# Attention kernel: a two-bank PSUM tile that is opened at step 3 and closed after the last step with three maxima, and another rotation of the late heads' banks

## The chip, the cores and the metric

The kernel runs on one core of a Trainium2 chip. The metric is the device time of one execution in microseconds (us); the median of three runs stands for a kernel. The core has TensorE (PE, matmuls; its weight loads are shown apart as PEld), VectorE (DVE), ScalarE (ACT, here the exponentials), GpSimd (POOL) and SyncE (SP, which issues the transfers). Matmul results land in PSUM, here used as eight banks of 128 partitions x 512 float32.

## The reference

Two attention blocks read the same x (2048 tokens, 448 features, 16 heads of 28) and a gate mixes them:

```python
g = _sigmoid((x * gate_w).sum(-1, keepdims=True))
a = _A_ref(x, A_wqkv, A_w_phi, A_wo)      # linear attention with a softmax feature map
b = _B_ref(x, B_wqkv, B_wo)               # below
return g * a + (1 - g) * b

# _B_ref
scores = jnp.einsum("bhqd,bhkd->bhqk", q, k) * scale
p = _softmax(scores, axis=-1)
o = jnp.einsum("bhqk,bhkd->bhqd", p, v)
return (o, heads joined) @ wo
```

All of it is float32, and the kernel keeps that precision by splitting numbers into a high and a low part.

## The kernel before

The first 350 us project x, do the linear attention of block A and prepare q, k and v of block B in device memory. The change touches none of that. From then on runs the softmax attention of block B, in 256 steps. A step s is one key tile of 128 tokens (kt, 16 of them) for one block of 512 queries (qb, 4 of them) of one group of four heads (g, 4 of them).

In a step PE computes, for the four heads, the scores transposed (128 keys x 512 queries), each in three passes that add into one PSUM bank (line 878, `score`: high x high, low x high, high x low). Each head uses 32 rows of the array, so matmuls of different heads run side by side. ACT takes the exponential of each finished bank (`exps_of`: line 887 for two banks at once, line 890 for one). Two steps later PE multiplies the exponentials with v (line 1033, `values`, the tile `pv`); that work uses the array in four column strips instead of four row strips.

The exponential needs a number per query to subtract. It is a maximum over keys, which is computed ahead of the group that needs it: further matmuls (line 288, `mx_score`), each with a reduction on DVE (line 295, `mx_done`). There are 704 of these, three in each of the steps 1 to 234 and two in step 235. From step 236 on a step has scores only. At six of the late steps (237, 239, 244, 246, 252, 254) PE also does two output projections, called pob (line 109 through `project`), each followed by one DVE instruction that adds the result into `acc` (line 1044). After step 255 the last block is finished in `finish_last`.

Eight banks are all there is. One holds `pv`. In before the other seven are five single tiles g2 to g6 and one tile named `wide` that is two banks; bank number 0 and bank number 1 in the code are its halves. All exist until the end of the kernel. In a step with three maxima the seven banks are given out in this order: two heads whose scores start first (e0 and e1), the first two maxima, two heads whose scores start later (l0 and l1), the third maximum. From step 2 on e0 and e1 have the two halves of `wide`, so that one exponential of 1024 columns serves both. The other five come from the list `ring`, which is permuted at every step. Step 1 runs on single exponentials, and one of its maxima is written into a half of `wide`. In the steps without three maxima, and for pob, the banks come from the front of the list `free`, so that halves of `wide` are used there one by one.

The order within a step is written out in `scores`: first pass of e0 and e1, the first two maxima; second pass of e0 and e1, first pass of l0 and l1; third pass of e0 and e1, second pass of l0 and l1; third pass of l0 and l1; the third maximum. Each engine works through its own queue in the order of the program. Semaphore waits are placed by the tile layer, per tile: a bank that is given out anew is a new tile and waits for the last reader of the old one, whereas `wide` is one tile for the whole kernel, and readers and writers of its halves are ordered as those of one object.

Of the kernel before, what the change touches and what calls it, by code (L numbers as in the profile page):

```python
# [8 lines left out]
F32 = mybir.dt.float32  # L9
# [5 lines left out]
PSUM = bass.MemoryType.PSUM  # L15
DRAM = bass.MemoryType.DRAM

P = 128
# [23 lines left out]
def gated_mix_kernel(ctx, tc, xT, wqkB, wvB, wvA, wkAT, wqAT, phi, woA, woB,  # L42
# [15 lines left out]
    ps = ps_s_.enter_context(tc.tile_pool(name="ps", bufs=1, space=PSUM, reuse_waits="tile"))  # L58
# [226 lines left out]
    def mx_score(item, pm):  # L285
        gq, kb, qt, j, _ = item
        js = slice(32 * j, 32 * j + DH)
        nc.tensor.matmul(pm, mxs[("qc", gq)][js, qt * P:(qt + 1) * P],  # L288
                         mxs[("kc", gq // NQ, kb)][js, :], start=True, stop=True,
                         tile_position=(32 * j, 0))  # L290

    def mx_done(item, pm):
        gq, kb, qt, h, col = item
        g, qb = divmod(gq, NQ)
        nc.vector.tensor_reduce(part[:, col:col + 1], pm, AX.X, ALU.max)  # L295
        if h < 3:
            return
        if kb == 1 and qt == 0 and gq + 1 < NG * NQ:
            mx_query(gq + 1)
        if qb == NQ - 1 and g + 1 < NG:  # L300
            if qt == 2 and kb == 3:
                mx_load(g + 1, 0)
            if qt == 3 and kb < 3:
                mx_load(g + 1, kb + 1)
        if qt == 3 and kb == 3:
            mx_reduce(gq)
# [404 lines left out]
    for i in range(2 * NT + 11):  # L711
# [15 lines left out]
        if q == 2:  # L727
# [7 lines left out]
            ps = ps_s_.enter_context(tc.tile_pool(name="psq", bufs=1, space=PSUM, reuse_waits="tile"))  # L735
# [18 lines left out]
        if q in (7, 10):  # L754
            b = 2 + q // 10
# [60 lines left out]
        if q == NT + 6:  # L816
            ps_s_.close()
            ps = ps_s_.enter_context(tc.tile_pool(name="psv", bufs=1, space=PSUM, reuse_waits="tile"))
# [51 lines left out]
    pv_of, pts, late, mids = {}, {}, {}, {}  # L870
    PASSES = ((0, 0), (1, 0), (0, 1))

    def score(s, j, n, st):

        gq, kt = divmod(s, NT)
        k, q = PASSES[n]
        js = slice(32 * j, 32 * j + 32)
        nc.tensor.matmul(st[j], kst_of[(gq // NQ, kt // 4)][js, k, (kt % 4) * P:(kt % 4 + 1) * P],  # L878
                         qst_of[gq][js, q, :], start=n == 0, stop=n == 2,
                         tile_position=(32 * j, 0), skip_group_check=True)  # L880

    def exps_of(s, js, st, wide=None):
        pw = late_p.tile([P, 2, 512], F32, tag="pw", name=f"pw{s}", bufs=4)
        pts[s] = {j: pw[:, i] for i, j in enumerate(js[:2])}
        pts[s].update({j: late_p.tile([P, 512], F32, tag="p", name=f"p{s}_{j}", bufs=8) for j in js[2:]})
        if wide is not None:
            nc.scalar.activation(pw, wide, AF.Exp, scale=SCALE)  # L887
            js = js[2:]
        for j in js:
            nc.scalar.activation(pts[s][j], st[j], AF.Exp, scale=SCALE)  # L890
# [11 lines left out]
    def scores(s, todo):  # L902

        if len(todo) == 3:
            l0, l1, e0 = [x[3] for x in todo]
            e1, = {0, 1, 2, 3} - {l0, l1, e0}
            order = [1, 2, 0, 3, 4, 5, 6] if s == 1 else [0, 1] + ring
            b = [bank(i, f"g{s}_{n}") for n, i in enumerate(order)]  # L910
            st, pm = {e0: b[0], e1: b[1], l0: b[4], l1: b[5]}, [b[2], b[3], b[6]]
            m0, m1, r0, r1, m2 = ring
            ring[:] = [3, 2, 6, 4, 5] if s == 1 else [m0, m1, r0, m2, r1]
            free[:] = [m0, m1, 0, 1, r0, m2, r1]
            for n in range(4):
                for j in (e0, e1) if n < 3 else ():
                    score(s, j, n, st)
                for i, j in enumerate((l0, l1)):
                    if n:
                        score(s, j, n - 1, st)  # L920
                    else:
                        mx_score(todo[i], pm[i])
            mx_score(todo[2], pm[2])
            js = [e0, e1, l0, l1]
        else:
            js = [0, 1, 2, 3]
            n = 4 + len(todo)
            b = free[:n]
            free[:] = free[n:] + b[4:] + b[:4]
            b = [bank(i, f"g{s}_{n}") for n, i in enumerate(b)]  # L930
            st, pm = dict(enumerate(b[:4])), b[4:]
            for n in range(3):
                for j in js:
                    score(s, j, n, st)
            for x, m in zip(todo, pm):
                mx_score(x, m)
        exps_of(s, js, st, wide if len(todo) == 3 and s > 1 else None)
        for x, m in zip(todo, pm):
            mx_done(x, m)

# [22 lines left out]
    take_acts()  # L963
    ps_s_.close()
    fr_s.close()
    ps2 = ctx.enter_context(tc.tile_pool(name="ps2", bufs=1, space=PSUM, reuse_waits="tile"))

    free, ring = [], [2, 3, 4, 5, 6]

    def bank(i, nm):
        if i < 2:
            return wide[:, i]
        return ps2.tile([P, 512], F32, tag=f"g{i}", name=nm, bufs=1)

    def take_bank(nm):
        free.append(free.pop(0))
        return bank(free[-1], nm)  # L980

    ps2.tile([P, 512], F32, tag="pv", name="pv_first", bufs=1)
    for i in (2, 6, 5, 4, 3):
        bank(i, f"first{i}")
    wide = ps2.tile([P, 2, 512], F32, tag="wide", name="wide", bufs=1)

    late_p = ctx.enter_context(tc.tile_pool(name="late", bufs=1, reuse_waits="tile"))
    woB_s = late_p.tile([P, 2, 4, D], F32R, name="woB_s")
# [37 lines left out]
    def values(s):  # L1026
        gq, kt = divmod(s, NT)
        g, qb = divmod(gq, NQ)
        if kt == 0:
            pv_of[gq] = ps2.tile([P, 512], F32, tag="pv", name=f"pv{gq}", bufs=1)  # L1030
        pv, pt = pv_of[gq], pts.pop(s)
        for j in range(4):
            nc.tensor.matmul(pv[32 * j:32 * j + 32, :], vb[kt // 8][:, kt % 8, 4 * g + j, :],  # L1033
                             pt[j],
                             start=kt == 0, stop=kt == NT - 1, tile_position=(0, 32 * j),
                             skip_group_check=True)
# [124 lines left out]
    for s in range(NS + 18):  # L1161
        gq, kt = divmod(s, NT)
        g, qb = divmod(gq, NQ)
# [18 lines left out]
        if 0 < s < NS:  # L1182
            if s in mids:
                mids.pop(s)()
            scores(s, mx_next())
# [4 lines left out]
        while vals and vals[0] <= upto:  # L1190
            t = vals.pop(0)
            values(t)
            if t % NT == NT - 1:
                finish(t // NT, s)
# [74 lines left out]
```

## Time and profile before

| what | us |
|---|---|
| median of 3 runs | 975.44 (975.02 to 976.71) |
| the profiled execution | 975.22 |
| its span | 973.4 |
| PE busy | 963.1 (99%) |
| ACT busy | 737.0 (76%) |
| DVE busy | 716.4 (74%) |
| POOL busy | 231.5 (24%) |

A timeline row gives start, duration, engine, line, operation, what is written and read, how many instructions are merged into the row, and in brackets how long the engine had been idle and what ended that. A releaser is inferred, and "issue" means that the engine waited for nothing that the profile shows. The profiled execution lies 0.22 us under the median, and 1.82 us of it lie outside the span.

### The profile page before, as it was taken

How to read it: one execution, taken by the hardware profiler on the slowest of the kernel's cores; microseconds unless marked ns; L12 is line 12 of the kernel's file. 1: busy time of each engine (PE TensorE's matmuls, PEld its weight loads, DVE VectorE, ACT ScalarE, POOL GpSimd, SP SyncE). 2: the span in 40 equal slices, each digit the busy share in tenths (PEclk: the TensorE clock that was granted, in tenths of full speed). 3: DMA queues.
4: the chain of work that ended last, by engine and by line, in shares of the span. 5: the costliest groups of instructions: out<-in, count | busy, mean ns of one | idle time of the engine just before them, and what ended most of it. 6: DMA issues, size and time to landing. Idle time of an engine off the chain costs nothing.

```text
span 973.4 us, 22367 instructions
## 1 busy us (share of the span) xinstructions
PE 963.1 (99%) x8510; PEld 573.3 (59%) x8510; DVE 716.4 (74%) x1338; ACT 737.0 (76%) x1209; POOL 231.5 (24%) x237
## 2 busy tenths in 40 slices
PE   9999999999999999999999999999999999999998
PEld 8877877787877654444444444444444444445555
DVE  5476767788845778888888888888888888884112
ACT  4465655588866788888888888888888888886561
POOL 1235435578634700121101101001101101100010
PEclk9999999999999999999999999999999999999999
DMA  9883111023233333022132022132132123000441
GB/s 301 307 266 118 36 54 33 35 62 87 85 107 104 110 107 125 22 59 60 51 103 72 22 62 60 51 87 73 51 84 60 51 59 94 13 21 31 151 144 57
DMA packets 56619, 84.48 MB, mean 87 GB/s; under 512 B 17696, under 2 KB 24464, under 8 KB 56512
## 3 DMA queue, kind: packets, MB, share of 16 engines
q1 hardware_dynamic: 56512, 83.06, 28.4%
q8 instruction: 67, 1.10, 0.5%
q14 instruction: 40, 0.33, 0.1%
HBM read 54.86 MB, written 27.78 MB: 85 GB/s over the span
## 4 chain that ended last, share of the span: by engine, by line
PE 99%; ACT 0%; DVE 0%; issue 0%; POOL 0%; DVEq 0%; POOLq 0%; ACTq 0%
PE pv L1033 26%; PE wide L878 18%; PE g L878 9%; PE pqk L109 6%; PE g L288 5%; PE poa L109 4%; PE pk L127 4%; PE pva L127 4%; PE pq L109 4%; PE pmd L260 4%; PE pvb L127 2%; PE pvb L109 2%; PE pob L109 2%; PE pft L521 2%; PE pqk L635 1%; PE wide L109 1%
## 5 line engine op out<-in xcount | busy, mean ns | idle before, releaser
L295 DVE TENSOR_REDUCE part<-g 128x1 f32<-128x512 f32 x703 | 441.8, 684 | 77.5 <-PE g L288 74.8
L887 ACT ACTIVATE pw<-wide 128x1024 f32<-128x1024 f32 x233 | 238.7, 1024 | 65.8 <-PE wide L878 64.6
L1033 PE MATMUL pv<-p,vb 128*32 128x512 f32 x1028 | 270.4, 604 | 0.0
L890 ACT ACTIVATE p<-g 128x512 f32<-128x512 f32 x495 | 269.2, 602 | 0.0
L1033 PE MATMUL pv<-pw,vb 128*32 128x512 f32 x1020 | 268.9, 604 | 0.0
L878 PE MATMUL g<-qst,kst 32*128 32x512 f32 x1587 | 245.7, 419 | 0.0
L878 PE MATMUL wide<-qst,kst 32*128 32x512 f32 x1473 | 240.8, 427 | 4.4 <-DVE acc L1044 1.7
L878 PEld LDWEIGHTS wide<-qst,kst 32*128 32x128 f32 x1473 | 119.6, 182 | 202.4 <-ACT pw L887 191.7
L288 PE MATMUL g<-kc,qc 28*128 28x512 f32 x703 | 231.8, 492 | 0.1
L878 PEld LDWEIGHTS g<-qst,kst 32*128 32x128 f32 x1587 | 128.3, 183 | 37.4 <-ACT pw L890 8.4
L265 DVE CUSTOM_DVE_ANT_0 rl<-pmb,rl 128x512 f32<-128x512 f32 x160 | 103.4, 684 | 50.7 <-ACT rl L264 50.7
L405 POOL TENSOR_TENSOR oUb<-oUb,rsb 128x512 f32<-128x512 f32 x15 | 19.3, 1287 | 488.6 <-DMA rsb<-rdb 356.8
L264 ACT ACTIVATE rl<-pmd 128x512 f32<-128x512 f32 x160 | 87.3, 601 | 31.1 <-PE pmb L260 29.6
L288 PEld LDWEIGHTS g<-kc,qc 28*128 28x128 f32 x703 | 86.4, 181 | 0.5 <-DVE part L295 0.4
L109 PE MATMUL pqk<-XH,wB 128*128 128x512 f32 x192 | 59.1, 396 | 0.0
L1033 PEld LDWEIGHTS pv<-pw,vb 128*32 128x32 f32 x1020 | 37.6, 108 | 36.1 <-issue 35.4
L1033 PEld LDWEIGHTS pv<-p,vb 128*32 128x32 f32 x1028 | 37.9, 108 | 31.8 <-issue 31.1
L573 ACT CAST ev<-pqk 128x512 fp32r<-128x512 f32 x28 | 16.0, 589 | 38.7 <-PE pqk L109 23.3
L109 PE MATMUL poa<-woA_s,oTa 128*128 128x448 f32 x192 | 43.4, 374 | 0.0
L574 DVE TENSOR_TENSOR ev<-pqk,ev 128x512 fp32r<-128x512 f32 x28 | 19.0, 689 | 30.7 <-ACT ev L573 30.7
L260 PE MATMUL pmb<-kp,qp 28*128 28x512 f32 x160 | 41.2, 495 | 0.0
L109 PEld LDWEIGHTS pqk<-XH,wB 128*128 128x128 f32 x192 | 35.4, 188 | 8.5 <-issue 1.2
(182 smaller groups left out, 1254.6 us busy)
## 6 DMA issues: line engine op xcount, KB each, us to landing
qkd<-ev SPq DMA_DIRECT2D x28, 512.0 KB
qst<-qkd SPq DMA_DIRECT2D x64, 112.0 KB
kst<-qkd SPq DMA_DIRECT2D x64, 112.0 KB
od<-oTb SPq DMA_DIRECT2D x48, 112.0 KB
rsa<-rda SPq DMA_DIRECT2D x32, 128.0 KB
oL<-od SPq DMA_DIRECT2D x8, 512.0 KB
rsb<-rdb SPq DMA_DIRECT2D x15, 256.0 KB
gad<-ga SPq DMA_DIRECT2D x16, 224.0 KB
```

What stands on the lines that cost most here:

```text
L109: nc.tensor.matmul(dst, l, r, start=i == 0, stop=i == len(todo) - 1)
L127: nc.tensor.matmul(dst[:, :n], l, r, start=i == 0, stop=i == len(todo) - 1, skip_group_check=True)
L260: nc.tensor.matmul(pm[j], qc[js, qt * P:(qt + 1) * P], kc[js, :], start=True, stop=True, tile_position=(32 * i, 0))
L264: nc.scalar.activation(rl, pm[i], AF.Relu)
L265: nc.vector.tensor_tensor_reduce(rl, pm[2 + i], rl, 1.0, LOWEST, ALU.add, ALU.max, part[:, col + i:col + i + 1])
L288: nc.tensor.matmul(pm, mxs[("qc", gq)][js, qt * P:(qt + 1) * P], mxs[("kc", gq // NQ, kb)][js, :], start=True, stop=True, tile_position=(3 ...
L295: nc.vector.tensor_reduce(part[:, col:col + 1], pm, AX.X, ALU.max)
L521: nc.tensor.transpose(p[:, (n - a) * P:(n - a + 1) * P], f[:, 2 * n:2 * n + 2].rearrange("p e c -> p (e c)"), ident)
L878: nc.tensor.matmul(st[j], kst_of[(gq // NQ, kt // 4)][js, k, (kt % 4) * P:(kt % 4 + 1) * P], qst_of[gq][js, q, :], start=n == 0, stop=n == ...
L887: nc.scalar.activation(pw, wide, AF.Exp, scale=SCALE)
L890: nc.scalar.activation(pts[s][j], st[j], AF.Exp, scale=SCALE)
L1033: nc.tensor.matmul(pv[32 * j:32 * j + 32, :], vb[kt // 8][:, kt % 8, 4 * g + j, :], pt[j], start=kt == 0, stop=kt == NT - 1, tile_position ...
```

## The change

The tile `wide` no longer exists from the start to the end. `pv` moves to a pool of its own (`ps1`). The other seven banks are in a pool that is opened three times by the new function `open_banks`: for steps 1 and 2 with seven single tiles, from step 3 with five single tiles and `wide` (now banks 3 and 2), and from step 235 with seven single tiles again. The order in which the first tiles are taken keeps each bank number at the same place in each of the pools.

Steps 1 and 2 have single exponentials for all four heads (one more step than before), and step 2 takes its banks from `free`. In the steps with `wide` the permutation of `ring` is another one. Before, l0 of a step got the bank that l0 had in the step before, l1 got that of the third maximum, and the third maximum that of l1. Now l0 gets the bank of the third maximum, l1 that of l0, and the third maximum that of l1, as before. The matmuls and their order in a step are the same; of the exponentials one pair becomes two single ones.

```diff
@@ scores(s, todo)
-            order = [1, 2, 0, 3, 4, 5, 6] if s == 1 else [0, 1] + ring
-            b = [bank(i, f"g{s}_{n}") for n, i in enumerate(order)]
+            if s == 3:
+                open_banks(3, True)
+            if s < 3:
+                b = free[:]
+                free[:] = [b[2], b[0], b[3], b[1], b[6], b[4], b[5]]
+            else:
+                b = [3, 2] + ring
+                m0, m1, r0, r1, m2 = ring
+                ring[:] = [m0, m1, m2, r0, r1]
+                free[:] = [m0, m1, 3, 2, m2, r0, r1]
+            b = [bank(i, f"g{s}_{n}") for n, i in enumerate(b)]
             st, pm = {e0: b[0], e1: b[1], l0: b[4], l1: b[5]}, [b[2], b[3], b[6]]
-            m0, m1, r0, r1, m2 = ring
-            ring[:] = [3, 2, 6, 4, 5] if s == 1 else [m0, m1, r0, m2, r1]
-            free[:] = [m0, m1, 0, 1, r0, m2, r1]
...
         else:
+            if banks["wide"] is not None:
+                open_banks(4, False)
...
-        exps_of(s, js, st, wide if len(todo) == 3 and s > 1 else None)
+        exps_of(s, js, st, banks["wide"] if len(todo) == 3 else None)
@@ after the first part of the kernel
-    ps2 = ctx.enter_context(tc.tile_pool(name="ps2", bufs=1, space=PSUM, reuse_waits="tile"))
-    free, ring = [], [2, 3, 4, 5, 6]
+    ps1 = ctx.enter_context(tc.tile_pool(name="ps1", bufs=1, space=PSUM, reuse_waits="tile"))
+    ps1.tile([P, 512], F32, tag="pv", name="pv_first", bufs=1)
+    free, ring = [0, 1, 2, 3, 4, 5, 6], [1, 0, 5, 6, 4]
+    banks = {}
+
+    def open_banks(n, pair):
+        if banks:
+            banks["s"].close()
+        banks.update(s=ctx.enter_context(ExitStack()), wide=None)
+        banks["ps"] = banks["s"].enter_context(
+            tc.tile_pool(name=f"ps{n}", bufs=1, space=PSUM, reuse_waits="tile"))
+        for i in (0, 6, 5, 4, 3, 2, 1):
+            if not pair or i not in (2, 3):
+                bank(i, f"first{n}_{i}")
+            elif i == 3:
+                banks["wide"] = banks["ps"].tile([P, 2, 512], F32, tag="wide", name="wide", bufs=1)
 
     def bank(i, nm):
-        if i < 2:
-            return wide[:, i]
-        return ps2.tile([P, 512], F32, tag=f"g{i}", name=nm, bufs=1)
+        if banks["wide"] is not None and i in (2, 3):
+            return banks["wide"][:, 3 - i]
+        return banks["ps"].tile([P, 512], F32, tag=f"g{i}", name=nm, bufs=1)
...
-    ps2.tile([P, 512], F32, tag="pv", name="pv_first", bufs=1)
-    for i in (2, 6, 5, 4, 3):
-        bank(i, f"first{i}")
-    wide = ps2.tile([P, 2, 512], F32, tag="wide", name="wide", bufs=1)
+    open_banks(2, False)
```

Three places in the instruction order show it. In the rows, g_0 to g_6 are the single tiles by their position in the step (a number behind the position only tells tiles apart), `kc` and `qc` are the operands of the maxima, `qst` and `kst` those of the scores, and the brackets name the engines whose semaphores the instruction waits for.

The first place is DVE at step 1, where it begins the reductions of the maxima. Before:

```order
L230 TENSOR_REDUCE red<-part 128x4x4 [waits DVE_49]
L857 STREAM_TRANSPOSE nm_4471<-red 128x128 [waits DVE_49]
L295 TENSOR_REDUCE part<-wide 128x1 [waits Activation_49]
L295 TENSOR_REDUCE part<-g_3_4474 128x1 [waits PE_49]
L295 TENSOR_REDUCE part<-g_6_4477 128x1 [waits PE_49]
```

And now:

```order
L230 TENSOR_REDUCE red<-part 128x4x4 [waits DVE_49]
L857 STREAM_TRANSPOSE nm_4475<-red 128x128 [waits DVE_49]
L295 TENSOR_REDUCE part<-g_2_4479 128x1 [waits PE_49]
L295 TENSOR_REDUCE part<-g_3_4480 128x1 [waits PE_49]
L295 TENSOR_REDUCE part<-g_6_4483 128x1 [waits PE_49]
```

The first maximum stood in a half of `wide` and its reduction waited for ACT; it now stands in a tile of its own and waits for PE.

The second place is PE in a step with three maxima in the middle of the attention: the first matmuls of step 233. Before:

```order
L878 MATMUL wide<-qst_4016,kst_4042 128x512 [waits Activation_49]
L878 MATMUL wide<-qst_4016,kst_4042 128x512
L288 MATMUL g_2_12711<-kc_2_9693,qc_11400 128x512 [waits DVE_49]
L288 MATMUL g_3_12712<-kc_2_9693,qc_11400 128x512 [waits DVE_49]
L878 MATMUL wide<-qst_4016,kst_4042 128x512 x2
L878 MATMUL g_4_12713<-qst_4016,kst_4042 128x512 [waits Activation_49]
L878 MATMUL g_5_12714<-qst_4016,kst_4042 128x512 [waits DVE_49]
```

And now:

```order
L878 MATMUL wide<-qst_4016,kst_4042 128x512 [waits Activation_49]
L878 MATMUL wide<-qst_4016,kst_4042 128x512
L288 MATMUL g_2_12730<-kc_2_9712,qc_11419 128x512 [waits DVE_49]
L288 MATMUL g_3_12731<-kc_2_9712,qc_11419 128x512 [waits DVE_49]
L878 MATMUL wide<-qst_4016,kst_4042 128x512 x2
L878 MATMUL g_4_12732<-qst_4016,kst_4042 128x512 [waits DVE_49]
L878 MATMUL g_5_12733<-qst_4016,kst_4042 128x512 [waits Activation_49]
```

The two late heads (g_4 is l0, g_5 is l1) have exchanged what they wait for; nothing else is moved.

The third place is PE at step 237, where the second of two projections is followed by the scores. Before:

```order
L109 MATMUL pob_12846<-woB_s,oTb_0_12292 128x448 [waits Pool_49]
L109 MATMUL wide<-woB_s,oL_11551 128x448 [waits Activation_49]
L109 MATMUL wide<-woB_s,oL_11551 128x448 x7
L109 MATMUL wide<-woB_s,oTb_0_12292 128x448 x3
L878 MATMUL wide<-qst_4016,kst_4018 128x512 [waits DVE_49]
L878 MATMUL g_1_12873<-qst_4016,kst_4018 128x512 [waits Activation_49]
```

And now:

```order
L109 MATMUL pob_12878<-woB_s,oTb_0_12311 128x448 [waits Pool_49]
L109 MATMUL pob_12892<-woB_s,oL_11570 128x448 [waits Activation_49]
L109 MATMUL pob_12892<-woB_s,oL_11570 128x448 x7
L109 MATMUL pob_12892<-woB_s,oTb_0_12311 128x448 x3
L878 MATMUL g_0_12906<-qst_4016,kst_4018 128x512 [waits Activation_49]
L878 MATMUL g_1_12907<-qst_4016,kst_4018 128x512 [waits Activation_49]
```

The first score had one half of `wide` while the projection had the other, and waited for DVE; it now has a tile of its own and waits for an exponential.

More of the change, by code (lines that the diff above doesn't have):

```diff
@@ L1029, in values @@
         if kt == 0:
-            pv_of[gq] = ps2.tile([P, 512], F32, tag="pv", name=f"pv{gq}", bufs=1)
+            pv_of[gq] = ps1.tile([P, 512], F32, tag="pv", name=f"pv{gq}", bufs=1)
         pv, pt = pv_of[gq], pts.pop(s)
```

## The prediction, made before the result

> **What bounds the kernel now.** I read the page first, then the waits of PE over the whole span, then the timelines of three places: the first steps, a step in the middle, and the last 90 us.
>
> ```profile
> span 973.4 us, 22367 instructions
> PE 963.1 (99%) x8510; PEld 573.3 (59%) x8510; DVE 716.4 (74%) x1338; ACT 737.0 (76%) x1209; POOL 231.5 (24%) x237
> PE 99%; ACT 0%; DVE 0%; issue 0%; POOL 0%; DVEq 0%; POOLq 0%; ACTq 0%
> ```
>
> PE carries 99% of the chain that ended last, and it is busy for all but 10.3 us. No matmul is removed, so the change can only fill gaps in PE or move the rhythm of the steps. These are the gaps that PE's own view names:
>
> ```profile
> PE wide L878 <- DVE acc L1044: 1.7, 2, 0.8
> ...
> PE wide L878 <- ACT p L890: 1.2, 1, 1.2
> PE wide L878 <- DVE part L295: 1.2, 1, 1.2
> PE wide L109 <- DVE acc L1044: 0.8, 1, 0.8
> PE wide L878 <- ACT pw L887: 0.3, 2, 0.2
> ```
>
> Columns are total us, times, longest. All five are matmuls that write the tile `wide`. Four of the five come where the change takes `wide` away: step 2 (DVE part) and the steps from 235 on (acc twice on line 878, once on line 109, and p). The weight loads show the gaps better, since there the length of an ordinary gap can be read too.
>
> **The start, steps 1 to 3.**
>
> ```profile
> 350.50 0.60 ACT L890 ACTIVATE pw<-wide 128x512 f32<-128x512 f32 x1
> 351.48 1.09 ACT L890 ACTIVATE p<-g 128x512 f32<-128x512 f32 x2
> 353.63 1.02 ACT L887 ACTIVATE pw<-wide 128x1024 f32<-128x1024 f32 x1 [1.06 <-PE wide L878]
> ...
> 349.52 0.50 PE L288 MATMUL g<-kc,qc 28*128 28x512 f32 x1
> ...
> 351.13 0.69 DVE L295 TENSOR_REDUCE part<-wide 128x1 f32<-128x512 f32 x1 [2.79 <-ACT pw L890]
> ...
> 351.88 0.18 PEld L878 LDWEIGHTS wide<-qst,kst 32*128 32x128 f32 x2 [1.60 <-DVE part L295]
> 353.98 0.16 PEld L1033 LDWEIGHTS pv<-p,vb 128*32 128x32 f32 x8 [0.37 <-PE wide L878]
> 354.97 0.18 PEld L878 LDWEIGHTS wide<-qst,kst 32*128 32x128 f32 x2 [0.84 <-ACT pw L887]
> 356.11 0.11 PEld L1033 LDWEIGHTS pv<-p,vb 128*32 128x32 f32 x2 [0.25 <-issue]
> ```
>
> The first maximum of step 1 is finished at about 350.02, yet its reduction starts at 351.13, just behind the exponential of the other half of `wide` (350.50 + 0.60 = 351.10). Step 2 needs that bank and loads its first weights at 351.82 + 0.06 = 351.88. After the change the reduction waits for PE alone, so it can start at about 350.1. Below, three reductions take 1.89, and a late head is released 0.05 behind its exponential. The last banks that step 2 needs are then set by ACT, whose exponentials of step 1 stay where they are: the one of l1 ends at 351.48 + 1.09 = 352.57 and frees the bank of step 2's third maximum, which starts at 352.62. The matmuls with v follow 0.42 behind a third maximum (below, 606.33 to 606.75): 353.04 instead of 353.98, a gain of 0.94. Step 3 then begins 0.94 earlier too, but now step 2 has four exponentials of one bank in place of one of 1.02 and two. They are 0.48 apart (two take 1.08, one 0.60). The first starts at about 352.9: l1 is released by l0's exponential of step 1 at 351.48 + 0.60 + 0.05 = 352.13, the third passes follow 0.20 later and last 0.50, and ACT is 0.1 behind them. The last ends at 352.9 + 3 x 0.48 + 0.60 = 354.94, frees the bank of step 3's third maximum at 354.99, and puts the matmuls with v of that step at 355.41 instead of 356.11, a gain of 0.70. Between 0.70 and 0.94 I take **0.8**, since both chains go on into the steps behind. ACT pays 0.18 once for the split (2 x 0.60 against 1.02), and that is in the 0.70.
>
> **The middle, steps 4 to 234.** A timeline of one step:
>
> ```profile
> 603.81 1.89 DVE L295 TENSOR_REDUCE part<-g 128x1 f32<-128x512 f32 x3 [0.48 <-PE g L288]
> ...
> 604.27 1.02 ACT L887 ACTIVATE pw<-wide 128x1024 f32<-128x1024 f32 x1 [0.32 <-PE wide L878]
> 605.19 1.08 ACT L890 ACTIVATE p<-g 128x512 f32<-128x512 f32 x2
> 606.54 1.02 ACT L887 ACTIVATE pw<-wide 128x1024 f32<-128x1024 f32 x1 [0.26 <-PE wide L878]
> ...
> 605.84 0.50 PE L878 MATMUL g<-qst,kst 32*128 32x512 f32 x2
> 606.04 0.39 PE L878 MATMUL wide<-qst,kst 32*128 32x512 f32 x2
> ...
> 606.33 0.49 PE L288 MATMUL g<-kc,qc 28*128 28x512 f32 x1
> 606.75 0.62 PE L1033 MATMUL pv<-pw,vb 128*32 128x512 f32 x2
> ...
> 883.02 1.02 ACT L887 ACTIVATE pw<-wide 128x1024 f32<-128x1024 f32 x1 [0.36 <-PE wide L878]
> ```
>
> From the double exponential at 353.63 to the last at 883.02 lie 232 steps, 2.282 us each. The rhythm is a circle through ACT. The exponential of l0 ends at 605.19 + 0.60 = 605.79 and l0 of the next step, in the same bank, starts at 605.84. Behind it in PE's queue stand the third passes of e0 and e1 (606.04 + 0.39 = 606.43), behind these the next double exponential (606.54), and 1.52 later l0's. That is 0.05 + 0.59 + 0.11 + 1.52 = 2.27. A second circle, over two steps, goes through l1's exponential, the third maximum (606.33), the matmuls with v and the next step, and is as long.
>
> The new rotation exchanges two waits. Before, l0 waits for ACT, and l1, next in the queue, for DVE's third reduction, which ends at 603.81 + 1.89 = 605.70. Now l0 waits for DVE and l1 for ACT. Whatever comes behind l1 still waits for the later of the two, and the third maximum still has l1's old bank. So the third passes start when they did, and I set the middle to **0**. The bounds: l1 no longer queues behind a held l0, which may save one place in the queue. Eight weight loads take 0.16 where one takes 0.11 (353.98), so a place is 0.007 us, times 231 steps 1.6 us; I allow as much the other way.
>
> **The end, from step 235.** Here are the gaps that end with `wide`, with ordinary ones beside them:
>
> ```profile
> 892.38 0.60 PEld L109 LDWEIGHTS wide<-woB_s,oTb 128*128 128x128 f32 x3
> 894.18 0.18 PEld L878 LDWEIGHTS wide<-qst,kst 32*128 32x128 f32 x1 [1.21 <-DVE acc L1044]
> ...
> 899.51 0.59 PEld L109 LDWEIGHTS pob<-woB_s,oTb 128*128 128x128 f32 x3
> 900.12 1.62 PEld L109 LDWEIGHTS pob<-woB_s,oL 128*128 128x128 f32 x8
> ...
> 902.65 0.19 PEld L878 LDWEIGHTS g<-qst,kst 32*128 32x128 f32 x3 [0.31 <-issue]
> ...
> 905.82 0.18 PEld L878 LDWEIGHTS wide<-qst,kst 32*128 32x128 f32 x1 [2.11 <-ACT p L890]
> ...
> 907.72 0.18 PEld L878 LDWEIGHTS g<-qst,kst 32*128 32x128 f32 x2 [0.84 <-issue]
> ...
> 927.52 0.18 PEld L878 LDWEIGHTS wide<-qst,kst 32*128 32x128 f32 x1 [1.22 <-DVE acc L1044]
> ...
> 950.72 1.51 PEld L109 LDWEIGHTS wide<-woB_s,oL 128*128 128x128 f32 x8 [1.23 <-DVE acc L1044]
> ...
> 893.45 0.68 DVE L1044 SCALAR_TENSOR_TENSOR acc<-wide,gate,acc 128x448 f32<-128x448 f32 x1 [1.62 <-PE wide L109]
> ...
> 903.71 1.08 ACT L890 ACTIVATE pw<-g 128x512 f32<-128x512 f32 x2 [4.50 <-PE g L878]
> ```
>
> Step 237 (894.18) is the pattern. Its first head takes bank 1, whose last exponential was two steps back. But the projection just before has bank 0, the other half, and the score starts 0.05 behind the end of DVE's addition (893.45 + 0.68 = 894.13). The ordinary gap between a projection and scores is 0.31 (902.65), so 1.21 - 0.31 = 0.90 goes. Step 246 (927.52) is the same: 0.91. At 254 (950.72) the second projection waits for the addition of the first; the ordinary gap there is 900.12 - (899.51 + 0.59) = 0.02, so 1.21 goes. At 240 (905.82) a score waits for an exponential of the other half; against 0.84 (907.72) it loses 1.27. The sum is 0.90 + 0.91 + 1.21 + 1.27 = **4.3**. If only the idle time in PE's own view went, it would be 1.7 + 0.8 + 1.2 = 3.7, which I keep as the end of the range.
>
> [...]
>
> What is late next? The list `free` hands out banks at the same distance as before, so I looked at what each step really needs. For step 240 that is the first exponential of step 239, which ends at 903.71 + 0.60 = 904.31, while PE would come at 905.82 - 1.27 = 904.55: 0.24 to spare. Opening the last pool costs nothing if each bank waits for its own last reader; the brackets in the order show one engine for each. No transfer and no POOL instruction is added or moved past another; those that the projections need hang on steps that come earlier by as much as the projections do.
>
> **Sum.** 0.8 + 0 + 4.3 = 5.1 us off the span: 968.3, an execution of 970.1, and with the 0.22 by which the median lies above the profiled execution, **970.3** (0.5%).
>
> **Rivals.**
> - *The rotation frees the rhythm.* l0 no longer waits for its own exponential. If l1's wait lay off the path, a step could shrink towards the shortest distances between double exponentials; 880.66 to 878.47 below is 2.19, so 231 x (2.282 - 2.19) = 21 us, 949. Against it: l1 takes over the same wait one place later. [...]
>
> ```profile
> 878.47 1.02 ACT L887 ACTIVATE pw<-wide 128x1024 f32<-128x1024 f32 x1 [0.63 <-PE g L288]
> 880.66 1.02 ACT L887 ACTIVATE pw<-wide 128x1024 f32<-128x1024 f32 x1 [0.18 <-PE wide L878]
> ```
>
> - *The rotation slows the rhythm.* l0, the earlier of the two in the queue, now hangs on DVE's third reduction, which has 605.84 - 605.70 = 0.14 in hand, and l0, l1 and the third maximum form one ring over three steps through both engines. With 0.05 lost per step it is 231 x 0.05 - 5.1 = +6.5, 982. It eats the gain from 0.022 per step, and is slower beyond the 0.2% from 0.031. Against it: before, l1 had the same wait at the same time.
> - *Closing a pool is a barrier.* Then step 3 waits for the last exponential of step 2 (354.94 instead of a start at 354.03, 0.9) and step 235 for that of 234 (883.02 + 0.92 + 1.08 = 885.02 against 884.13, 0.9). The time is 972.1. Against it: the brackets.
>
> ```profile
> 884.13 0.18 PEld L878 LDWEIGHTS g<-qst,kst 32*128 32x128 f32 x2 [0.84 <-DVE part L295]
> ```
>
> - *The end has another wait behind the false ones.* Four single exponentials are 0.48 apart, 1.9 a step, as long as a step of PE without maxima (905.82 to 907.72). If that takes back half of the end, 972.5.
> - *Nothing moves*, 975.4: the waits were named wrongly and others end at the same time.
>
> **Chances.** The forecast 0.70, rhythm freed 0.04, rhythm slowed 0.09, barrier 0.07, other wait 0.05, nothing 0.05. What a measurement of this kernel can tell from no change is about 0.2%, 1.95 us. Faster: 0.70 + 0.04 + 0.07 + 0.05 = 0.86; same 0.05; slower 0.09. The range: the early end is 970.3 less 1.6 of the middle and 0.7 for runs, 968.0; the late end holds the barrier and the other wait, 972.7. Together 0.82.
>
> **What would show it.** After the change no matmul on line 878 or 109 waits for acc, and the waits of PE on line 878 for DVE part are gone or shorter than 0.5. The distance of double exponentials stays within 0.007 of 2.28, and the first is at about 355.2 in the time of the trace. From the last double exponential to the end there are about 4.3 us less than 973.4 - 883.02 = 90.4. The prediction is wrong if the step changes by 0.02, or if the 90 us shrink by less than 3.

## The result, and the profile after

The changed kernel takes 969.79 us (median of 6 runs, 969.22 to 970.2); the kernel before, run beside it, takes 975.75 (6 runs, 975.02 to 976.71). The ratio is 0.9937, with a 95% interval of 0.9924 to 0.995: 0.6% faster. The forecast was 970.3 with a range from 968.0 to 972.7.

The page of the profile after, and under it everything that PE's view of waits still names over the whole span:

```profile
span 968.0 us, 22373 instructions
PE 962.7 (99%) x8510; PEld 592.2 (61%) x8510; DVE 716.0 (74%) x1338; ACT 737.0 (76%) x1210; POOL 230.9 (24%) x237
...
PE pqk L618 <- POOL ident masks.py:199: 1.4, 1, 1.4
PE wide L878 <- ACT pw L887: 0.2, 1, 0.2
```

The span is 5.4 shorter, and PE's busy time is nearly what it was (962.7 against 963.1): the gaps went, not the work. The waits for `acc`, the one for DVE's `part` and the one for `p` are gone; 0.2 is left in the attention.

Two marks divide the span, the first double exponential that both kernels have (step 3) and the last one (step 234). Between them lie 231 steps. ACT's timeline of the changed kernel has them at:

```profile
355.08 1.02 ACT L887 ACTIVATE pw<-wide 128x1024 f32<-128x1024 f32 x1 [0.32 <-PE wide L878]
...
881.70 1.02 ACT L887 ACTIVATE pw<-wide 128x1024 f32<-128x1024 f32 x1 [0.36 <-PE wide L878]
```

| stretch | before | after | difference | forecast |
|---|---|---|---|---|
| to the double exponential of step 3 | 355.98 | 355.08 | -0.90 | -0.8 |
| 231 steps | 527.04 (2.2816 each) | 526.62 (2.2797 each) | -0.42 | 0 |
| from the last double exponential to the end | 90.38 | 86.30 | -4.08 | -4.3 |
| span | 973.4 | 968.0 | -5.4 | -5.1 |

The stretch before step 1 is equally long in the two traces (the four exponentials of step 0 start at 347.96 and 347.97). In the other kept traces these four start anywhere from 347.19 to 348.99, so below the parts of a span are compared, not the spans.

**The start.** DVE, ACT and the weight loads at steps 1 to 3:

```profile
350.13 3.76 DVE L295 TENSOR_REDUCE part<-g 128x1 f32<-128x512 f32 x6 [1.77 <-PE g L288]
...
350.53 1.09 ACT L890 ACTIVATE pw<-g 128x512 f32<-128x512 f32 x2
352.69 1.08 ACT L890 ACTIVATE pw<-g 128x512 f32<-128x512 f32 x2
353.67 1.10 ACT L890 ACTIVATE p<-g 128x512 f32<-128x512 f32 x2
...
350.88 0.48 PEld L878 LDWEIGHTS g<-qst,kst 32*128 32x128 f32 x2 [0.58 <-DVE part L295]
352.07 0.60 PEld L878 LDWEIGHTS g<-qst,kst 32*128 32x128 f32 x8 [0.22 <-DVE part L295]
353.06 0.16 PEld L1049 LDWEIGHTS pv<-p,vb 128*32 128x32 f32 x8 [0.24 <-PE g L878]
355.24 0.11 PEld L1049 LDWEIGHTS pv<-p,vb 128*32 128x32 f32 x2 [0.24 <-issue]
```

The reduction starts at 350.13 instead of 351.13, now behind PE, and six reductions run without a break. PE's gap ahead of step 2 is 0.58 instead of 1.60. The matmuls with v of step 2 stand at 353.06 (forecast 353.04) and those of step 3 at 355.24 (forecast 355.41).

**The end.** The weight loads at the four places of the forecast, in the order of time:

```profile
891.96 0.54 PEld L878 LDWEIGHTS g<-qst,kst 32*128 32x128 f32 x12 [0.32 <-issue]
...
902.32 0.53 PEld L878 LDWEIGHTS g<-qst,kst 32*128 32x128 f32 x12 [0.84 <-ACT pw L890]
...
923.11 0.54 PEld L878 LDWEIGHTS g<-qst,kst 32*128 32x128 f32 x12 [0.29 <-issue]
...
944.54 0.60 PEld L109 LDWEIGHTS pob<-woB_s,oTb 128*128 128x128 f32 x3
945.16 1.61 PEld L109 LDWEIGHTS pob<-woB_s,oL 128*128 128x128 f32 x8
947.69 0.53 PEld L878 LDWEIGHTS g<-qst,kst 32*128 32x128 f32 x12 [0.29 <-issue]
```

The gaps of 1.21, 2.11, 1.22 and 1.23 are now 0.32, 0.84, 0.29 and 0.02 (945.16 less 944.54 + 0.60), the lengths that the forecast called ordinary.

### The profile page after: what moved, and what is told of

It is laid out like the page before. It is cut to its first block, busy times and chain, and to the rows that moved or that the text cites. A ratio compares the mean times of both kernels' runs of the same rounds, so it can differ in the third digit from the quotient of the medians.

```text
span 968.0 us, 22373 instructions
## 1 busy us (share of the span) xinstructions
PE 962.7 (99%) x8510; PEld 592.2 (61%) x8510; DVE 716.0 (74%) x1338; ACT 737.0 (76%) x1210; POOL 230.9 (24%) x237
## 4 chain that ended last, share of the span: by engine, by line
PE 99%; DVE 0%; ACT 0%; POOL 0%; issue 0%; POOLq 0%
PE pv L1049 27%; PE wide L878 18%; PE g L878 11%; PE pqk L109 6%; PE poa L109 4%; PE pk L127 4%; PE pva L127 4%; PE pq L109 4%; PE g L288 4%; PE pmd L260 4%; PE pob L109 3%; PE pvb L127 2%; PE pvb L109 2%; PE pft L521 2%; PE pqk L635 1%; PE pn L534 1%
## 5 line engine op out<-in xcount | busy, mean ns | idle before, releaser
L890 ACT ACTIVATE p<-g 128x512 f32<-128x512 f32 x510 | 277.9, 606 | 0.0
L878 PE MATMUL g<-qst,kst 32*128 32x512 f32 x1668 | 250.2, 412 | 0.1
L878 PEld LDWEIGHTS wide<-qst,kst 32*128 32x128 f32 x1392 | 112.1, 182 | 194.8 <-ACT pw L887 190.6
L878 PE MATMUL wide<-qst,kst 32*128 32x512 f32 x1392 | 224.7, 426 | 0.2 <-ACT pw L887 0.2
L878 PEld LDWEIGHTS g<-qst,kst 32*128 32x128 f32 x1668 | 158.6, 183 | 22.9 <-ACT pw L890 10.9
L890 ACT ACTIVATE pw<-g 128x512 f32<-128x512 f32 x46 | 26.3, 654 | 27.9 <-PE g L878 27.7
L1060 DVE SCALAR_TENSOR_TENSOR acc<-pob,gate,acc 128x448 f32<-128x448 f32 x12 | 8.2, 684 | 48.0 <-PE pob L109 48.0
```

## The experiments

All are changes to the changed kernel. Each is timed against the kernel before on the same chip (medians of before from 975.53 to 975.71). delay_l0, delay_l1, dve_short and spare_short were executed once, the others four to ten times. This table has the marks of their traces; what follows from them stands under each.

| kernel | step 3 | last double exponential | us per step | from there to the end | time, us |
|---|---|---|---|---|---|
| before | 355.98 | 883.02 | 2.2816 | 90.38 | 975.75 |
| after | 355.08 | 881.70 | 2.2797 | 86.30 | 969.79 |
| old_rotation | 354.29 | 881.26 | 2.2813 | 86.34 | 969.67 |
| pair_to_end | 355.82 | 882.40 | 2.2796 | 90.5 | 973.94 |
| start_as_before | 356.59 | 883.16 | 2.2795 | 86.24 | 971.3 |
| fill_gap | 355.98 | 882.54 | 2.2795 | 86.26 | 970.56 |
| pool_waits | 355.54 | 882.06 | 2.2793 | 87.24 | 971.37 |
| e_passes_first | 355.36 | 881.94 | 2.2796 | 86.26 | 969.36 |
| delay_l0 | 355.26 | 899.26 | 2.3550 | 86.54 | 987.58 |
| delay_l1 | 356.08 | 899.78 | 2.3537 | 86.72 | 988.26 |
| dve_short | 354.56 | 880.29 | 2.2759 | 86.51 | 968.53 |
| spare_bank | 354.93 | 867.87 | 2.2205 | 86.23 | 956.04 |
| spare_short | 355.05 | 851.97 | 2.1512 | 86.23 | 939.99 |

### The three parts of the change, undone one by one

The rotation of before in the changed kernel:

```diff
-                ring[:] = [m0, m1, m2, r0, r1]
-                free[:] = [m0, m1, 3, 2, m2, r0, r1]
+                ring[:] = [m0, m1, r0, m2, r1]
+                free[:] = [m0, m1, 3, 2, r0, m2, r1]
```

> The changed kernel with the rotation of before. Theory (the new rotation only exchanges the waits of l0 and l1): 969.8 within 0.5, a step of 2.2816 as before instead of 2.2797, so 0.4 us more at most; start and end as in the changed kernel (first double exponential at 355.08, 86.3 us from the last one to the end). Rival (the rotation frees or slows the rhythm, and something else hides it): more than 2 us in either direction.

Measured: 969.67 (969.38 to 970.15), ratio to before 0.9939 (0.9925 to 0.9954). A step is 2.2813, so 0.0016 longer than with the new rotation, 0.4 us over 231 steps, which the times cannot show. The rotation is worth next to nothing by itself, in either direction.

The pair kept to the end:

```diff
-            if banks["wide"] is not None:
-                open_banks(4, False)
             js = [0, 1, 2, 3]
```

> The changed kernel without the opening of the last pool, so that the pair lasts to the end of the kernel. Theory (the end's gain is the four false waits on the other half of the pair): 973.9, that is 4.1 us more, with single waits for acc and for an exponential back at steps 237, 240, 246 and 254; the steps before 235 unchanged. Rival (the end's gain came from the other rotation of the banks in the list free, or from the pool): within 1 us of 969.8.

Measured: 973.94 (973.5 to 974.72), ratio 0.9981 (0.9971 to 0.999); 4.15 more than the changed kernel, and 4.2 of it behind the last double exponential (90.5 against 86.30). PE's waits are those of before again:

```profile
PE wide L878 <- DVE acc L1058: 1.7, 2, 0.8
...
PE wide L878 <- ACT p L890: 1.2, 1, 1.2
PE wide L109 <- DVE acc L1058: 0.8, 1, 0.8
```

So the end's gain comes from the pair alone: the new rotation and the new bank numbers are in this kernel too, and without the reopened pool the four holds are back.

The start of before:

```diff
-            if s == 3:
-                open_banks(3, True)
-            if s < 3:
-                b = free[:]
-                free[:] = [b[2], b[0], b[3], b[1], b[6], b[4], b[5]]
+            if s == 1:
+                b = [3, 1, 2, 0, 4, 5, 6]
+                ring[:] = [0, 1, 6, 4, 5]
...
-        exps_of(s, js, st, banks["wide"] if len(todo) == 3 else None)
+        exps_of(s, js, st, banks["wide"] if len(todo) == 3 and s > 1 else None)
...
-    open_banks(2, False)
+    open_banks(2, True)
```

> The changed kernel with the pair open from step 1, the first maximum of step 1 in one half and the double exponential from step 2, as before. Theory: 0.9 us more (970.7), the reduction of the first maximum again behind an exponential at about 351.1, and all of it in the first three steps. Rival (the start's gain is lost or made up again in the steps behind it): within 0.3 us of 969.8.

Measured: 971.3 (971.03 to 972.57), ratio 0.9958 (0.9943 to 0.9973): 1.5 more, not 0.9. The trace has the reduction of the first maximum behind an exponential again, and then something that neither kernel's profile had shown. The stretches of this trace, with the granted TensorE clock in the column PEclk:

```profile
core 0: us, PE busy (x) PEld busy (x) DVE busy (x) ACT busy (x) POOL busy (x), PEclk, DMA share, GB/s
350.00:353.00 3.00, 1.78 (x15) 0.96 (x15) 2.62 (x5) 1.94 (x5) 0.00 (x0) 1.00 0.40 133
353.00:354.00 1.00, 1.00 (x13) 0.16 (x8) 1.00 (x2) 1.00 (x2) 0.00 (x0) 0.72 0.38 115
354.00:355.00 1.00, 1.00 (x12) 0.10 (x4) 0.14 (x1) 0.87 (x2) 0.00 (x0) 0.50 0.60 141
355.00:356.00 1.00, 1.00 (x12) 0.81 (x15) 0.23 (x1) 0.00 (x0) 0.00 (x0) 0.50 0.29 97
356.00:357.00 1.00, 1.00 (x15) 0.35 (x11) 1.00 (x2) 0.41 (x1) 0.00 (x0) 0.57 0.03 4
```

PE is idle for 1.22 of the three us from 350. Then the clock is at 0.50 in the two us from 354, at 0.72 in the one before and at 0.57 in the one behind. If 0.72 and 0.57 are means of 1.00 and 0.50, with one change in each of these two us, the low clock lasts about 3.4 us, from 353.44 to 356.86, an estimate from these rows. In that time one step takes 3.7 instead of 2.3 (double exponentials at 352.87 and 356.59). The next run asks whether the wait brings the low clock.

The same start, with matmuls in PE's wait (each on all 128 rows of the array, 128*128 in the profile; nobody reads the result):

```diff
+        if s == 2:
+            pf = ps1.tile([P, 512], F32, tag="pv", name="pv_fill", bufs=1)
+            for _ in range(4):
+                nc.tensor.matmul(pf, kst_of[(0, 0)][:, 0, :P], qst_of[0][:, 0, :], start=True, stop=True)
         if 0 < s < NS:
```

> The start as before (pair from step 1), but with four matmuls of 128 x 512 whose result nobody reads, put where PE waits ahead of step 2. In the start as before, the granted TensorE clock fell to 0.50 from about 353.6 to 357, behind PE's wait of 1.6 ahead of step 2, and took some 1.5 us. Theory (the wait brings the low clock): no low clock any more, a median of 970.7 to 971.0, that is the 0.9 of the start alone. Rival (the low clock has another cause): the low clock stays in most executions, median 971.3 or more.

Measured: 970.56 (970.25 to 971.26), ratio 0.995 (0.9936 to 0.9964), with a granted clock of 1.0 in each of the five executions. Step 2 waits as long as before (its first scores at 351.88, behind DVE), but PE's longest gap there is now 0.47:

```profile
350.66 0.76 PEld L1199 LDWEIGHTS pv_fill<-qst,kst 128*128 128x128 f32 x4 [0.37 <-ACT vb L699]
351.88 0.18 PEld L878 LDWEIGHTS wide<-qst,kst 32*128 32x128 f32 x2 [0.47 <-DVE part L295]
```

So the start is worth 0.8 by itself (970.56 - 969.79; 0.90 by the traces), and in some executions the low clock comes on top: three of the four of start_as_before had a mean granted clock of 0.997 or 0.998, none of the five of fill_gap. Of the 29 executions of the kernel before beside these experiments, 15 had a mean granted clock of 0.998 and a mean time of 976.12, and 13 had 1.00 and 975.26. That is 0.86 in half of the executions. All six of the changed kernel were at 1.0, and so were all ten of pair_to_end, which has the end of before: it belongs to the start. Two things are not shown. The kept trace of before is one at 1.0, so it does not say where its clock falls; and the times of start_as_before do not price the low clock by themselves, since its one execution at 1.0 took 971.03 and the others 971.18 to 972.57.

### What opening a pool costs

```diff
-            tc.tile_pool(name=f"ps{n}", bufs=1, space=PSUM, reuse_waits="tile"))
+            tc.tile_pool(name=f"ps{n}", bufs=1, space=PSUM, reuse_waits="tile" if n == 2 else "pool"))
```

> The changed kernel, but each opening of the pools at steps 3 and 235 waits for all users of the pool that is closed, instead of bank by bank. Theory: 0.9 us at each of the two places, 971.6 in all, 1.8 more; the first scores of step 3 and of step 235 start just behind the last exponential of the step before. Rival (other waits hide it): within 0.4 us of 969.8.

Measured: 971.37 (970.76 to 971.79), ratio 0.9954 (0.9938 to 0.9971), 1.58 more than the changed kernel. The two openings, at steps 3 and 235:

```profile
354.49 0.18 PEld L878 LDWEIGHTS wide<-qst,kst 32*128 32x128 f32 x2 [1.59 <-ACT p L890]
...
884.11 0.54 PEld L878 LDWEIGHTS g<-qst,kst 32*128 32x128 f32 x12 [1.77 <-ACT p L890]
```

The gaps are 0.75 and 0.93 longer than the 0.84 of the changed kernel. With waits bank by bank the trace shows no cost at either opening; as barriers they would have taken back more than a quarter of the gain.

### What sets the step

The forecast named two circles as equally long. The first goes through l0's exponential and the third passes of e0 and e1, the second over two steps through l1's exponential and the third maximum. The first is cut by another order of PE's queue:

```diff
-            for n in range(4):
-                for j in (e0, e1) if n < 3 else ():
-                    score(s, j, n, st)
-                for i, j in enumerate((l0, l1)):
-                    if n:
-                        score(s, j, n - 1, st)
-                    else:
-                        mx_score(todo[i], pm[i])
+            for j in (e0, e1):
+                score(s, j, 0, st)
+            for i in range(2):
+                mx_score(todo[i], pm[i])
+            for n in (1, 2):
+                for j in (e0, e1):
+                    score(s, j, n, st)
+            for n in range(3):
+                for j in (l0, l1):
+                    score(s, j, n, st)
             mx_score(todo[2], pm[2])
```

> The changed kernel with the third passes of e0 and e1 ahead of the first passes of l0 and l1 in PE's queue. Theory (the rhythm is the circle l0's exponential, next step's late heads, third passes of e0 and e1, double exponential): the circle is cut, a step goes from 2.28 towards the shortest distances of 2.19, and the time to about 950 to 956. Rival (PE itself sets the step; a round in which the late heads' rows are idle adds 0.1 to 0.2): a step of 2.3 to 2.4 and 975 to 998.

Measured: 969.36 (968.83 to 970.01), ratio 0.9936 (0.9921 to 0.9951), a step of 2.2796: both expectations fell. The circle is cut and nothing comes of it, so it did not hold the step by itself. (With a second circle of the same length, a cut of the first would change nothing either; the delays below decide.) Nor did PE lose a round. A step of that trace; the third passes are the last loads into `wide`:

```profile
604.73 1.08 ACT L890 ACTIVATE p<-g 128x512 f32<-128x512 f32 x2
...
605.86 0.18 PEld L288 LDWEIGHTS g<-kc,qc 28*128 28x128 f32 x1
...
607.39 0.19 PEld L878 LDWEIGHTS wide<-qst,kst 32*128 32x128 f32 x2
607.43 0.30 PEld L878 LDWEIGHTS g<-qst,kst 32*128 32x128 f32 x2
607.63 0.18 PEld L878 LDWEIGHTS wide<-qst,kst 32*128 32x128 f32 x2
```

The late heads' first weights (607.43) go in ahead of the third passes (607.63), though they stand behind them in the queue. What remains is the third maximum: it starts at 605.86, 0.05 behind the end of l1's exponential (604.73 + 1.08 = 605.81). That is the second circle, and two runs lengthen each circle by the same ACT instruction, put ahead of l0's exponential (i == 0) or between l0's and l1's (i == 1):

```diff
-        for j in js:
+        for i, j in enumerate(js):
+            if wide is not None and i == 0:
+                nc.scalar.copy(dly[:, 1], dly[:, 0])
             nc.scalar.activation(pts[s][j], st[j], AF.Exp, scale=SCALE)
```

> The changed kernel with one more ACT instruction (a copy of 160 columns, about 0.18 by the rows of 512 and 1024 columns) between the double exponential and l0's. Theory of the first circle (one step long, through l0's exponential): +0.18 per step, +42 us. Second circle alone (two steps long, through l1's exponential): +0.09 per step, +21 us. Neither (ACT has 2.28 - 1.88 = 0.40 free in a step): 0.

> The same copy between l0's and l1's exponentials. First circle alone: 0, since it does not go through l1's. Second circle (l1's exponential, third maximum, v matmuls, next step): it is passed once in two steps, +0.09 per step, +21 us.

Measured: 987.58 and 988.26, steps of 2.3550 and 2.3537. ACT in the first of the two:

```profile
604.80 1.03 ACT L887 ACTIVATE pw<-wide 128x1024 f32<-128x1024 f32 x1
605.73 0.32 ACT L891 COPY dly<-dly 128x160 f32<-128x160 f32 x1
605.94 1.09 ACT L892 ACTIVATE p<-g 128x512 f32<-128x512 f32 x2
```

The copy puts l0's exponential off by 0.21 (605.94 - 605.73). The step grows by 0.075 and 0.074, the same at both places. Through the first circle the first place would give 0.21 and the second 0; through the second both give half of it, 0.105. So of the two it is the second that holds. Some 0.03 of the 0.105 is missing. In the traces between 360 and 850 us the third maximum starts less than 0.07 behind the end of an exponential in 171 of the 214 steps of the changed kernel whose maxima are all recorded, and in all 207 of delay_l0; a circle that does not hold in every step would fit the missing part, but no run tests it. Here it is in the changed kernel, from l1's exponential of one step to that of two steps later:

```profile
604.48 1.08 ACT L890 ACTIVATE p<-g 128x512 f32<-128x512 f32 x2
608.10 1.02 ACT L887 ACTIVATE pw<-wide 128x1024 f32<-128x1024 f32 x1 [0.31 <-PE wide L878]
609.02 1.08 ACT L890 ACTIVATE p<-g 128x512 f32<-128x512 f32 x2
...
605.61 0.50 PE L288 MATMUL g<-kc,qc 28*128 28x512 f32 x1
606.04 0.62 PE L1049 MATMUL pv<-pw,vb 128*32 128x512 f32 x2
607.04 0.49 PE L878 MATMUL wide<-qst,kst 32*128 32x512 f32 x2
607.60 0.40 PE L878 MATMUL wide<-qst,kst 32*128 32x512 f32 x2
```

l1's exponential ends at 605.56; 0.05 later the third maximum takes its bank (605.61); 0.43 later, behind it in the queue, the matmuls with v (606.04); 1.00 later the next step (607.04), 0.56 later its third passes (607.60), 0.50 later the double exponential (608.10), and 2.00 later the end of l1's (610.10). The sum is 4.54 for two steps, 2.27 each, beside a measured 2.2797. It has to come out at two steps, since it runs from an event to the same event two steps later; that the circle holds is shown by the delays, not by the sum.

DVE is no part of that circle. To see whether it matters since the new rotation gives l0 the bank of DVE's third reduction:

```diff
-            mx_done(x, m)
+            mx_done(x, m[:, :128] if len(todo) == 3 and s > 2 else m)
```

> The changed kernel, but from step 3 on the reductions of the steps with three maxima read 128 of the 512 columns (the maxima are over a quarter of the keys), so that DVE leaves each bank some 0.4 earlier. Theory (the step closes through ACT: the third maximum's bank comes from l1's exponential, and l1's own from l0's): 2.28 and 969 to 970, even though l0 now takes the bank that DVE's third reduction leaves. Rival (since the new rotation, DVE's third reduction is what holds the step): a step of 2.25 or less, 963 or less.

Measured: 968.53, a step of 2.2759, 0.0038 shorter. A reduction alone takes 0.29 now, where a full one alone takes 0.69, and that changes next to nothing:

```profile
605.21 0.29 DVE L295 TENSOR_REDUCE part<-g 128x1 f32<-128x128 f32 x1 [0.32 <-PE g L288]
```

So the place behind DVE, which l0 has since the new rotation, is not what sets the step.

Last, the cause is taken away: one bank to spare.

```diff
-                ring[:] = [m0, m1, m2, r0, r1]
+                ring[:] = [m0, r1, m1, m2, r0]
                 free[:] = [m0, m1, 3, 2, m2, r0, r1]
-            b = [bank(i, f"g{s}_{n}") for n, i in enumerate(b)]
+            b = [bank(i, f"g{s}_{n}") if s < 3 or n != 3 else None for n, i in enumerate(b)]
+            b[3] = b[3] if s < 3 else b[2]
...
-                    else:
+                    elif s < 3 or i == 0:
                         mx_score(todo[i], pm[i])
```

> The changed kernel without the matmul of the second maximum in the steps with the pair (its reduction reads the first maximum's bank again, so a third of the maxima is not computed); the bank that this frees goes into the rotation, so that no late head and no maximum gets a bank that an exponential has just left. Theory (the step is set by the circle through the bank of l1's exponential): a step falls from 2.28 to PE's own 2.17 to 2.19 and the time to 944 to 950. Rival (PE's or ACT's own work sets the step): 2.28 and 969 to 970, since the matmul left out runs beside others and DVE and ACT do what they did.

Measured: 956.04 (955.29 to 956.24), ratio 0.9799 (0.9786 to 0.9812), a step of 2.2205. The step falls, but only 0.059 of the 0.09 to 0.11 expected. The trace has a new wait in the next place. DVE's reductions and the late heads' loads of one step:

```profile
605.45 1.89 DVE L295 TENSOR_REDUCE part<-g 128x1 f32<-128x512 f32 x3 [0.60 <-PE g L288]
...
607.13 0.44 PEld L878 LDWEIGHTS g<-qst,kst 32*128 32x128 f32 x2
```

The two loads stretch over 0.44, so the second starts at 607.57 - 0.18 = 607.39, 0.05 behind the end of the third reduction (607.34), whose bank l1 has in this rotation. With a shorter reduction in the place of the second maximum:

```diff
-        for x, m in zip(todo, pm):
-            mx_done(x, m)
+        for i, (x, m) in enumerate(zip(todo, pm)):
+            mx_done(x, m[:, :64] if len(todo) == 3 and s > 2 and i == 1 else m)
```

> The kernel with the spare bank, and the reduction that stands in for the second maximum cut to 64 of 512 columns (a third of the maxima is not computed). Theory (with the spare bank the step stopped at 2.22 because l1 takes the bank of the third maximum and waits for DVE's third reduction): 2.15 to 2.19, 940 to 948. Rival (PE's own work in a step is 2.22): 954 as with the spare bank.

Measured: 939.99, a step of 2.1512. Double exponentials follow each other at an even distance, 2.14 and 2.15:

```profile
604.77 1.02 ACT L887 ACTIVATE pw<-wide 128x1024 f32<-128x1024 f32 x1 [0.16 <-PE g L878]
606.91 1.02 ACT L887 ACTIVATE pw<-wide 128x1024 f32<-128x1024 f32 x1
609.06 1.02 ACT L887 ACTIVATE pw<-wide 128x1024 f32<-128x1024 f32 x1
```

So in the changed kernel some 0.13 of each step, 30 us in all (231 x (2.2797 - 2.1512) = 29.7; the time fell by 29.8), is waiting for banks: 0.059 goes with the spare bank, the rest only when DVE's reduction is shortened as well. That PE has a matmul less per step in these two kernels is not what makes the steps short. The first and second passes of a step of spare_short start 0.34 apart (605.85 and 606.19), those of the changed kernel 0.33 (607.04 and 607.37), and the changed kernel, with all its matmuls, has single steps of 2.16 (first passes at 525.08 and at 527.25, 2.163 before rounding). The two kernels do not compute a third of the maxima, so they are no versions of the kernel; they price one bank more. Of the kernels that do all the work, e_passes_first (969.36) and the changed kernel (969.79) cannot be told apart.

## Why the prediction was right, step by step

- **The start, -0.8.** Measured -0.90 in the traces and 0.8 between fill_gap and the changed kernel. The chain to step 2's matmuls with v came out at 0.02 of the forecast. Step 3 gained 0.87, within 0.70 to 0.94, though one leg of its chain was wrong. l1's first weights went in at 352.15, behind l0's exponential as forecast (352.13), but the third passes of e0 and e1 followed at 352.16 and not 0.20 later, so step 2's exponentials started at 352.69 and not at 352.9. The 0.20 had been read from the middle (605.84 to 606.04), where it is not an answer to the late heads' release: there the third passes follow their own second passes (605.81). What the forecast did not have is the low clock: 0.86 in the half of the executions of before that had a mean granted clock of 0.998. It fits that the medians lie 5.96 apart and the traces, both at full clock, only 5.4.
- **The middle, 0 with bounds of 1.6.** Measured -0.42, the rotation's part of it 0.4 (old_rotation). The number was right, one of its two reasons was not. The first circle, 0.05 + 0.59 + 0.11 + 1.52, is no circle that closes: the 0.59 counted from l0's start to the end of the third passes, as if these followed l0. In that step they follow their own second passes (605.81 to 606.04), so l0's release at 605.84 had 0.2 in hand; cutting the link gave nothing (e_passes_first), nor did a delay on it count in full (delay_l0: 0.075 of 0.21). The second circle, which the forecast mentioned in one sentence, is the one that holds (delay_l0 and delay_l1 alike, spare_bank). Both circles gave 0, so the wrong one cost the forecast nothing, and that was luck. The new rotation leaves it as it was, since the third maximum still has l1's old bank.
- **The end, -4.3.** Measured -4.08. The four places gave 0.90 (steps from 235 to 237 lie 2.22 earlier instead of 1.32), 1.28, 0.92 and 1.21, which is the forecast's sum. 0.16 was lost at the last pair of projections: 0.06 ahead of it, and 0.10 since the loads of a projection that need not wait take 1.61 instead of the 1.51 behind a wait; the 0.07 still missing is not placed. Undoing the last opening cost 4.15. The measured value lies between the forecast and its low bound of 3.7, nearer to the forecast.
- **The holds are of the program's making.** The 4.3 needs that a score can run while DVE reads another bank. After the change it does: the matmuls of step 237's scores run from 891.96 to 892.94, and DVE's addition of the projection, from another bank, starts within them at 892.07. With the pair kept to the end the holds are back (pair_to_end, 4.15 more):

```profile
891.96 0.98 PE L878 MATMUL g<-qst,kst 32*128 32x512 f32 x12
892.07 0.68 DVE L1060 SCALAR_TENSOR_TENSOR acc<-pob,gate,acc 128x448 f32<-128x448 f32 x1 [1.56 <-PE pob L109]
```

- **The rivals.** The pool as a barrier was priced at 1.8 and costs 1.58 when it is one (pool_waits); here it is none. The rhythm was neither freed nor slowed. For "freed", one bank more to rotate into is worth 0.059 per step (spare_bank; 0.13 in spare_short, with the shorter reduction as well); the one other permutation of the same five that was run gives 0.0016.
- **What would show it.** The waits on `acc` are gone, as is DVE's `part` from PE's view; double exponentials moved by 0.0019 each, the first is at 355.08 for about 355.2, and the stretch to the end shrank by 4.08, above the 3 set as the limit.

## What to carry to other kernels

If one tile spans two banks, a part of the program that uses the halves singly can pay for it with waits that no data asks for (4.15 us here, at the end); let the pair exist only where it is used as a pair, and close and open the pool with waits bank by bank (as barriers the two openings cost 1.58). To say what a new rotation gives, follow the chain from each release to the next use until it closes, and test a supposed circle by cutting or delaying one link: of two circles that sum to the same time only one may hold. Here, with every bank in use, the other permutation was worth 0.4 us and one free bank 13.75 (969.79 to 956.04).

## What the runs showed of the hardware that was not expected

- **A wait of PE was followed by a low clock.** In start_as_before, 1.22 us of PE's idle time between 350 and 353 were followed by about 3.4 us (the estimate above) with a granted clock of 0.50. With matmuls in that wait the clock was 1.0 in all five executions (fill_gap), against one of four without them. The idle time alone does not decide it: in the kept trace of before PE is idle for 1.25 of the same three us, and the clock stays at 1.00. What else it takes was not shown:

```profile
core 0: us, PE busy (x) PEld busy (x) DVE busy (x) ACT busy (x) POOL busy (x), PEclk, DMA share, GB/s
350.00:353.00 3.00, 1.75 (x21) 0.71 (x13) 1.86 (x3) 2.52 (x6) 0.00 (x0) 1.00 0.46 129
353.00:354.00 1.00, 1.00 (x15) 0.52 (x13) 1.00 (x3) 0.37 (x1) 0.00 (x0) 1.00 0.47 137
354.00:355.00 1.00, 1.00 (x14) 0.16 (x12) 0.90 (x2) 1.00 (x2) 0.00 (x0) 1.00 0.45 150
355.00:356.00 1.00, 1.00 (x19) 0.82 (x15) 0.45 (x1) 0.65 (x3) 0.00 (x0) 1.00 0.47 111
356.00:357.00 1.00, 1.00 (x11) 0.16 (x8) 1.00 (x3) 1.00 (x2) 0.00 (x0) 1.00 0.06 12
```

- **Matmuls in other rows overtook.** With the third passes of e0 and e1 ahead of the late heads' first passes in PE's queue (e_passes_first), the late heads' loads came first (607.43 against 607.63), their matmuls started first (607.63 against 607.86), and the step did not become a round longer (2.2796):

```profile
607.63 0.42 PE L878 MATMUL g<-qst,kst 32*128 32x512 f32 x2
607.86 0.40 PE L878 MATMUL wide<-qst,kst 32*128 32x512 f32 x2
```

So that an engine works through its queue in the order of the program does not hold for the starts of these matmuls: those of the late heads, in rows of their own, started 0.23 ahead of third passes that stand before them in the queue (607.63 and 607.86).
